# Pooled attention and a squared-ReLU layer: the first pair's fp32 scores of two heads in row halves, the weight conversion spread over three engines, one-piece splits and a new written order

## The chip, the cores and the metric

The kernel runs on one core of a Trainium2 chip. The metric is the device time of one execution in microseconds (us). The core has five engines that the text speaks of: PE (TensorE, matrix products), ACT (ScalarE), DVE (VectorE), POOL (GpSimd) and SP (SyncE, which here only starts DMA transfers). Each of them works through its own instructions in the order in which the program lists them.

## What is computed

```python
# q, k, v: (4, 8, 1152, 64); w_in: (512, 2048); w_out: (2048, 512); all float32
q_pool = q.reshape(B, H, S // 2, 2, D).mean(axis=3)
scores = scale * np.matmul(q_pool, k.transpose(0, 1, 3, 2))
scores = scores - np.max(scores, axis=-1, keepdims=True)
attn = np.exp(scores)
attn = attn / (np.sum(attn, axis=-1, keepdims=True) + 1e-09)
attn_out = np.matmul(attn, v)
x = attn_out.transpose(0, 2, 1, 3).reshape(B * 576, 512)   # 2304 tokens
r = np.maximum(x @ w_in, 0.0)
out = (r * r) @ w_out
```

## The kernel before

**Attention.** The 32 heads are worked on as 16 pairs, four pairs to a batch. A pair has 9 chunks of 128 query rows: four of each head, and one (the fifth) that holds the last 64 rows of both. There are 144 chunks, numbered from 0 in the order in which they are worked on. For a chunk `i` the steps are named: `S` (PE: scores, 128 x 1152, into one of two score tiles `s0` and `s1`, chosen by `i % 2`), `MX` (DVE: maximum of each row, L678), `EX` (ACT: exponential with row sums, L689 and L690, three instructions), and then the turning of the 128 x 1152 weights for the next product. In the first batch (chunks 0 to 35) that is `TP`, three groups of three transposes on PE (L738) into one of two PSUM banks `ba`, each followed by a copy out of the bank, `TC`, on ACT (L750) or DVE (L752). In the later batches a chunk is split into a high and a low fp16 part (`HI`, `LO`, L694 to L702) and turned by DMA (`TR`), or turned on PE (L788 to L811). `PV` multiplies with the values (L854 in fp32 for the first batch, L863 in fp16), and `ED` copies the result out.

**A pair's operands.** The keys and queries of a pair come by DMA (`LK`, `LQ`), get a scale (`GR`, `GM`, `GF`, `GS`, `GT`, `GU`, `GW`, `GE`), are split into fp16 parts (`KA` and `KD` for keys, `QA` and `QD` for queries, `VA` and `VD` for values), and are turned by DMA (`KT`, `QT`). `QX` (L588) copies the turned queries into the other half of the partitions, in two instructions of 64 partitions. `QS` adds neighbouring queries. Pair 0 alone is worked on in fp32: its keys and queries are turned on PE (`KX`, `QY`), and its scores are products with a contraction over 64 partitions, partitions 0 to 63 for the first head and 64 to 127 for the second (L649).

**Weights.** The two weight matrices are loaded in 16 pieces (`WL`, L1107) and converted, piece by piece, by bit operations: `W1` (L1113) and `W2` (L1118) on ACT, `W3` (L1122) and `W5` (L1126) on DVE, `W4` (L1135) on POOL or DVE. `WG`, `WM` and `WS1` to `WS3` find the scale of a matrix, `WA`, `WB` and `WD` split it into fp16 parts.

**The layer behind it.** When a block of 256 tokens is done, it is scaled and split (`RV` to `XD`) and goes through eight `H` (PE, L1005), with `HA`, `G1`, `G2`, `G3` on the other engines, and eight `O` (PE, L1054). There are nine blocks.

**The order.** Nothing is scheduled on the chip. A planner (class `Plan`) places all these steps one after the other on the five engines, from a table of durations, an offset for each kind of step and a few weights, all in `CFG` and `COST`. Where a step may go to two or three engines (`alt`, with the table `ALT`), the planner also picks the engine. The order that comes out is the program.

```python
ORD = [0, 1, 7, 8, 2, 3, 4, 5, 6]     # chunks of a pair: heads 0, 0, 1, 1, 0, 0, both, 1, 1
add(("S", i), {"PE": 2050}, ... + back, scores4, i)    # back: EX of chunk i - 2
add(("W1", c), {"ACT": 1030}, [("WL", c)] + wx, w1, at)
add(("QX", n), alt("QX", DVE=1100, POOL=2500), [("QT", n)] + old, qx, need)
```

## Time and profile before

| what | value |
|---|---|
| time of the kernel, median of 3 runs | 863.12 us (855.28 to 863.9) |
| time of the profiled execution | 867.78 us |
| its span, first to last instruction | 866.0 us |
| mean granted TensorE clock | 0.953 |
| PE busy | 786.8 us, 91% of the span |
| DVE busy | 629.5 us, 73% |
| ACT busy | 582.7 us, 67% |
| POOL busy | 373.4 us, 43% |

The span is 1.8 us shorter than the profiled execution's own time. That execution lies 4.7 us above the median of the runs. A share of busy time is a mean over the program: the chunks end at about 712 us, and behind that nearly only PE works. A clock of 1.00 in a stretch means that PE was granted 2.4 GHz, and 0.50 means 1.2 GHz. A busy time of PE at the lower level is longer for the same work.

### The profile page before, as it was taken

Reading aid. Unit: us, or ns where it says so; the run is one execution under the profiler, and the core shown is the slowest. Engines: PE = TensorE matmul, PEld = TensorE weight load, DVE = VectorE, ACT = ScalarE, POOL = GpSimd, SP = SyncE. Lnnn points to the kernel's source line nnn. Section 1 sums busy time; section 2 is a strip of 40 time slices with the busy share of each in tenths; the row PEclk is TensorE's granted clock in tenths of the full one; section 3 lists DMA queues with packets and bytes.
Section 4 is the critical chain, followed back from the end, with each engine's and each line's share of the span. In section 5 each row is a group of like instructions: output and inputs, shape, how many; then the busy total and the mean of one; then the engine's idle time right before and its main releaser. Section 6 shows DMA issues by size and latency. Waiting matters only on the chain. (4 is left out here: it accounts for less than half of the span.)

```text
span 866.0 us, 15480 instructions
## 1 busy us (share of the span) xinstructions
PE 786.8 (91%) x6106; PEld 517.2 (60%) x6106; DVE 629.5 (73%) x782; ACT 582.7 (67%) x953; POOL 373.4 (43%) x261
## 2 busy tenths in 40 slices
PE   6988878887799989898999898999989989999997
PEld 4555545454586557555765574577557646857573
DVE  2678999898978888888885988888888892413120
ACT  4567879599975678767884865588658872725150
POOL 2233332337676557444782556665357641000000
PEclk8669999898899999998999999899999999999999
DMA  9457953334787889797978987989989976000001
GB/s 286 126 139 193 251 164 125 85 98 93 125 150 149 169 180 184 150 196 135 203 123 187 195 159 161 181 153 179 171 175 182 183 136 108 2 13 13 13 13 25
DMA packets 296489, 120.72 MB, mean 139 GB/s; under 512 B 279776, under 2 KB 279776, under 8 KB 296416
## 3 DMA queue, kind: packets, MB, share of 16 engines
q1 hardware_dynamic: 296416, 119.73, 67.5%
q8 instruction: 48, 0.79, 0.4%
q14 instruction: 25, 0.20, 0.1%
HBM read 45.09 MB, written 4.72 MB: 58 GB/s over the span
## 5 line engine op out<-in xcount | busy, mean ns | idle before, releaser
L678 DVE TENSOR_REDUCE ca<-s 128x1 f32<-128x1152 f32 x144 | 193.0, 1349 | 28.4 <-PE s L670 17.4
L1005 PEld LDWEIGHTS <-w 128*128 128x128 f16 x1728 | 168.5, 98 | 31.4 <-issue 5.5
L690 ACT ACTIVATE buf<-s,ca,esc 128x1152 f32<-128x1152 f32 x135 | 177.0, 1311 | 6.9 <-POOL buf L702 0.3
L702 POOL TENSOR_TENSOR buf<-buf,buf 128x1152 f16<-128x1152 f32 x55 | 139.2, 2534 | 58.5 <-ACT buf L694 35.6
L1054 PE MATMUL ba<-w,region 128*128 128x512 f16 x672 | 153.3, 382 | 1.0 <-ACT ru L908 1.0
L670 PE MATMUL s<-kT,qT 128*128 128x512 f16 x720 | 138.9, 333 | 10.5 <-ACT buf L690 10.3
L1054 PEld LDWEIGHTS <-region 128*128 128x128 f16 x864 | 83.7, 99 | 96.8 <-issue 4.9
L1005 PE MATMUL ba<-region,w 128*128 128x256 f16 x1104 | 128.4, 275 | 2.4 <-DVE PT L811 1.8
L670 PEld LDWEIGHTS <-qT 128*128 128x128 f16 x720 | 64.9, 100 | 68.6 <-issue 21.3
L863 PE MATMUL ba<-PT,v 128*64 128x320 f16 (+1 forms) x1296 | 88.5, 296 | 6.3 <-DVE PT L811 3.2
L1032 DVE TENSOR_TENSOR region<-region 128x512 f16<-128x512 f32 x42 | 39.3, 936 | 69.3 <-ACT region L1025 68.7
L863 PEld LDWEIGHTS <-v 128*64 128x64 f16 x1296 | 74.6, 114 | 19.8 <-issue 12.6
L689 ACT ACTIVATE ca<-ca,cols,esc 128x1 f32<-128x1 f32 x135 | 51.4, 381 | 50.1 <-DVE ca L678 49.8
L702 DVE TENSOR_TENSOR buf<-buf,buf 128x1152 f16<-128x1152 f32 x41 | 64.7, 1578 | 9.6 <-ACT buf L694 5.9
L738 PE MATMUL ba<-ident,buf 128*128 128x128 f32 x324 | 56.8, 306 | 16.2 <-DVE PT L752 8.0
L349 POOL TENSOR_SCALAR buf<-buf,cols 128x1152 f16<-128x1152 f32 x31 | 43.6, 1407 | 52.8 <-ACT buf L690 36.7
L352 DVE SCALAR_TENSOR_TENSOR buf<-raw,psc,buf 128x576 f16<-128x576 f32 x45 | 55.7, 1272 | 3.4 <-POOL buf L326 3.4
L738 PEld LDWEIGHTS ba<-ident,buf 128*128 128x128 f32 x324 | 37.8, 153 | 33.5 <-DVE PT L752 13.7
L1032 POOL TENSOR_TENSOR region<-region 128x512 f16<-128x512 f32 x30 | 42.4, 1414 | 34.0 <-ACT region L1025 31.8
L750 ACT ACTIVATE PT<-ba 128x384 f32<-128x384 f32 (+1 forms) x73 | 31.1, 454 | 27.5 <-PE ba L738 27.0
L1005 PE MATMUL bt<-region,w 128*128 128x256 f16 x432 | 49.2, 273 | 0.0
L1135 POOL TENSOR_TENSOR w<-w,region 128x1024 f32<-128x1024 f32 x11 | 26.5, 2410 | 52.2 <-DVE w L1126 50.0
(158 smaller groups left out, 1112.0 us busy)
## 6 DMA issues: line engine op xcount, KB each, us to landing
raw<-in_k_dram SPq DMA_DIRECT2D x16, 576.0 KB, 4.6
raw<-in_q_dram SPq DMA_DIRECT2D x32, 288.0 KB, 4.4
region<-in_moe_w_in_dram SPq DMA_DIRECT2D x8, 1024.0 KB, 6.0
region<-in_moe_w_out_dram SPq DMA_DIRECT2D x8, 1024.0 KB, 5.4
raw<-in_v_dram SPq DMA_DIRECT2D x12, 576.0 KB, 4.5
out_dram<-buf SPq DMA_DIRECT2D x36, 128.0 KB, 2.4
v<-in_v_dram SPq DMA_DIRECT2D x4, 576.0 KB, 5.5
PT<-buf SPq DMA_TRANSPOSE x108, 4.8
```

Source lines behind the costliest of these rows:

```text
L349: nc.gpsimd.tensor_scalar(out, x, s0, s1, op0=ALU.mult, op1=ALU.mult)
L352: nc.vector.scalar_tensor_tensor(out=o, in0=x, scalar=s, in1=h, op0=ALU.mult, op1=ALU.subtract)
L670: nc.tensor.matmul(s[:, x, :w], lhsT=qt[:, l, h, c0 : c0 + 2, :].rearrange("p a b -> p (a b)"), rhs=rhs, **st)
L678: nc.vector.reduce_max(a[:, 0:1], st3(), axis=AX.X)
L689: nc.scalar.activation(a[:, 1:2], a[:, 0:1], AF.Identity, bias=ln14, scale=s0)
L690: nc.scalar.activation(P(), st3(), AF.Exp, bias=a[:, 1:2], scale=s1, accum_out=col)
L702: e.tensor_tensor(out=hl()[:, 1], in0=P(), in1=hl()[:, 0], op=ALU.subtract)
L738: nc.tensor.matmul(t[:, y], lhsT=P()[:, c * 128 : (c + 1) * 128], rhs=ident, is_transpose=True, start=(y == 0), stop=(y == 2), skip_group_ ...
L863: nc.tensor.matmul(px[h * 64 : (h + 1) * 64, :N], lhsT=vv[:, h, kc, vl, :], rhs=t[:, 9 * pl + kc, :N], start=(i == 0), stop=(i == 3 * NC - ...
L1005: nc.tensor.matmul(ph[:, f2], lhsT=w16[0][:, SLOT[f // 4], wl, a, f % 4 * 128 : (f % 4 + 1) * 128], rhs=xhl()[:, xl, a], start=(i == 0), s ...
L1032: e.tensor_tensor(out=gt[u][:, 1], in0=rt[u % 2], in1=gt[u][:, 0], op=ALU.subtract)
L1054: nc.tensor.matmul(p[:, :DM], lhsT=g[:, gl, f % 2, tt * 128 : (tt + 1) * 128], rhs=w16[1][:, SLOT[f // 4], wl, f % 4], start=(f == 0 and g ...
```

## The change

**Scores of pair 0.** The chunks of pair 0 are taken in the order `ORD4`, in which each two neighbours belong to different heads, and one `S` now computes two chunks: its matrix products alternate between partitions 0 to 63, into `s0`, and 64 to 127, into `s1`. The fifth chunk stays alone. The joint `S` waits for the `EX` of two earlier chunks, since it writes both score tiles.

**Weight conversion.** `W1` may go to ACT or POOL, `W2` to ACT or DVE. On DVE `W2` is a bit operation on 16-bit words.

**Splits.** `KD`, `VD` and `QX` were steps of two instructions each; each instruction is now a step that is placed by itself, and the two halves of a `QX` may go to different engines.

**Order.** `CFG` and `COST` hold other numbers, so the planner's whole order is another one. The rest of the diff (operands kept in a buffer, `PART`, visits) is not used with this `CFG`.

How many steps of a kind stand on an engine, where the two programs differ by three or more:

| step | before | after |
|---|---|---|
| `S` of pair 0 | PE 9 | PE 5 |
| `W1` | ACT 16 | POOL 16 |
| `W2` | ACT 16 | ACT 12, DVE 4 |
| `W4` | POOL 14, DVE 2 | POOL 11, DVE 5 |
| `TC` | ACT 65, DVE 43 | ACT 83, DVE 25 |
| `QX`, instructions | DVE 30 | DVE 15, POOL 15 |
| `KA` | POOL 11, ACT 4 | POOL 4, ACT 11 |
| `VA` | ACT 8, POOL 4 | ACT 3, POOL 9 |
| `HI` | ACT 41, POOL 31, DVE 24 | ACT 44, POOL 24, DVE 28 |
| `G2` | ACT 49, POOL 13, DVE 10 | ACT 64, POOL 2, DVE 6 |
| `G3` | DVE 42, POOL 30 | DVE 27, POOL 45 |
| `ED` | ACT 23, DVE 9 | ACT 20, DVE 12 |

```diff
-ALT = {"TC": "D", "KC": "D", ...}
+ALT = {"W1": "P", "W2": "D", "TC": "D", "KC": "D", ...}
...
+    def both(i):
+        n, _, vi = chunks[i]
+        if n not in full_s:
+            return (i,)
+        x = i - visits[vi][2]
+        y = i if x == 4 else i - (x - (x > 4)) % 2
+        return (i,) if x == 4 else (y, y + 1)
...
         def scores4(o):
-            s = sts[i % 2]
...
-                nc.tensor.matmul(
-                    s[:, x, :w], lhsT=qt[hs, cs].rearrange("p a b -> p (a b)"),
-                    rhs=kt[hs, k0:k1].rearrange("p a b -> p (a b)"), start=True, stop=True,
-                )
+                for y in both(i):
+                    ch = CH[chunks[y][1]]
...
+                    nc.tensor.matmul(
+                        sts[y % 2][:, x, :w], lhsT=qt[hs, cs].rearrange("p a b -> p (a b)"),
+                        rhs=kt[hs, k0:k1].rearrange("p a b -> p (a b)"), start=True, stop=True,
+                    )
...
         if n in full_s:
-            add(("S", i), {"PE": 2050}, ... + back, scores4, i)
+            if both(i)[0] == i:
+                back = [("EX", y - 2) for y in both(i) if y >= 2]
+                add(("S", i), {"PE": 2200 if len(both(i)) == 2 else 2050}, ... + back, scores4, i)
...
-            add(("KD", n), {"DVE": 1500}, [("KA", n)], kd, need, give=("k", n))
+            for h in range(2):
+                add(("KD", n, h), {"DVE": 730}, [("KA", n)] + ..., lambda o, h=h: kd(o, h), need, ...)
...
-            add(("QX", n), alt("QX", DVE=1100, POOL=2500), [("QT", n)] + old, qx, need)
+            for z in range(2):
+                add(("QX", n, z), alt("QX", DVE=470, POOL=1500), [("QT", n)] + old, lambda o, z=z: qx(o, z), need)
...
                     def w1(o, w=w, i=i, half=half, c=c):
-                        nc.scalar.activation(
-                            f32(w, i)[:, half], wst[c % 2][:, :, :, 1].bitcast(F32), AF.Copy, scale=2.0 ** -112
-                        )
+                        to, x = f32(w, i)[:, half], wst[c % 2][:, :, :, 1].bitcast(F32)
+                        if o["eng"] == "ACT":
+                            nc.scalar.activation(to, x, AF.Copy, scale=2.0 ** -112)
+                        else:
+                            pmul(to, x, 2.0 ** -112)
 
                     def w2(o, c=c):
-                        nc.scalar.activation(wsg[c % 2], wst[c % 2][:, :, :, 1].bitcast(F32), AF.Sign)
+                        if o["eng"] == "ACT":
...
+                            e.tensor_scalar(
+                                wsg[c % 2].bitcast(I16), wst[c % 2].bitcast(I16)[:, :, :, 3], -(2 ** 15), 0x3F80,
+                                op0=ALU.bitwise_and, op1=ALU.bitwise_or,
+                            )
...
-                    add(("W1", c), {"ACT": 1030}, [("WL", c)] + wx, w1, at)
+                    add(("W1", c), alt("W1", ACT=1030, POOL=1250), [("WL", c)] + wx, w1, at)
...
+    ORD4 = [0, 7, 1, 8, 4, 2, 5, 3, 6]
```

Three places show how the order moves. The first is PE at the start: `L442` is the last of the queries' turning, `s0_113` and `s1_114` are the two score tiles, and the rows behind are the first scores. Before:

```order
L442 MATMUL ba0_115<-ident_81,raw1_101 64x64 x8
L649 MATMUL s0_113<-kT0_102,qT0_104 128x512 x2
L649 MATMUL s0_113<-kT0_102,qT0_104 128x128
L649 MATMUL s1_114<-kT0_102,qT0_104 128x512 x2
L649 MATMUL s1_114<-kT0_102,qT0_104 128x128
```

After, where `L677` is the same line:

```order
L459 MATMUL ba0_115<-ident_81,raw1_101 64x64 x8
L677 MATMUL s0_113<-kT0_102,qT0_104 128x512
L677 MATMUL s1_114<-kT0_102,qT0_104 128x512
L677 MATMUL s0_113<-kT0_102,qT0_104 128x512
L677 MATMUL s1_114<-kT0_102,qT0_104 128x512
L677 MATMUL s0_113<-kT0_102,qT0_104 128x128
L677 MATMUL s1_114<-kT0_102,qT0_104 128x128
```

The two tiles were filled one after the other by two steps; they are now filled in turn by one.

The second is DVE about chunk 14, in the first batch: `L588` and `L604` are `QX`, `L1122` and `L1161` are `W3`, `L1126` and `L1165` are `W5`, `L1135` is `W4`, `L678` and `L706` are `MX`, `L356` is a half of `KD`. Before:

```order
L588 COPY qT_104<-qT_104 64x1152 x2
L521 TENSOR_SCALAR psc<-psc 128x2
L1126 SCALAR_TENSOR_TENSOR region<-region 128x1024
L528 TENSOR_SCALAR psc<-psc 128x2
L1135 TENSOR_TENSOR region<-region 128x1024
L534 RECIPROCAL psc<-psc 128x2
L1166 TENSOR_REDUCE wsc<-ba_115 128x1
L678 TENSOR_REDUCE ca<-s_114 128x1
```

After:

```order
L706 TENSOR_REDUCE ca<-s_113 128x1
L356 SCALAR_TENSOR_TENSOR buf_97<-raw_101,psc,buf_97 128x9x64
L706 TENSOR_REDUCE ca<-s_114 128x1
L1161 TENSOR_SCALAR region<-region 128x1024
L604 COPY qT_104<-qT_104 64x1152
L1165 SCALAR_TENSOR_TENSOR region<-region 128x1024
```

One of the two copies of `QX` has left DVE here, `W4` has left it in this place, and a half of `KD` stands between two `MX`.

The third is POOL from the first `QS` (`L407` and `L423`) on: `L353` with a `w` behind it is `W1`, `L1135` and `L1174` are `W4`, `L349` is `GE`, `L326` is `KA` and `QA`, `L604` is a half of `QX`. Before:

```order
L407 TENSOR_TENSOR raw_101<-raw_101 128x9x64
L1135 TENSOR_TENSOR w_0_90<-w_0_90,region 128x1024
L407 TENSOR_TENSOR raw_101<-raw_101 128x9x64
L349 TENSOR_SCALAR esc<-psc 128x1 x2
L326 TENSOR_SCALAR buf_96<-raw_100,psc 128x18x64
L326 TENSOR_SCALAR buf_97<-raw_101,psc 128x9x64
L1135 TENSOR_TENSOR w_0_90<-w_0_90,region 128x1024 x3
```

After:

```order
L423 TENSOR_TENSOR raw_101<-raw_101 128x9x64
L353 TENSOR_SCALAR w_0_90<-region 128x1024
L1174 TENSOR_TENSOR w_0_90<-w_0_90,region 128x1024
L353 TENSOR_SCALAR w_0_90<-region 128x1024
L423 TENSOR_TENSOR raw_101<-raw_101 128x9x64
L353 TENSOR_SCALAR w_0_90<-region 128x1024
L353 TENSOR_SCALAR esc<-psc 128x1 x2
L1174 TENSOR_TENSOR w_0_90<-w_0_90,region 128x1024
L353 TENSOR_SCALAR w_0_90<-region 128x1024 x2
L1174 TENSOR_TENSOR w_0_90<-w_0_90,region 128x1024
L604 COPY qT_105<-qT_105 64x1152
```

The first pieces of `W1` and a half of `QX` now stand between `QS`, `GE` and `W4`; `KA` and `QA` of pair 1 have left POOL.

## Rows read from the trace of the kernel before

**Rows 1.** By stretch: us; busy of PE, PEld, DVE, ACT, POOL; PEclk; DMA; GB/s:

```profile
0.00:58.95 58.95, 49.61 (x224) 30.29 (x224) 29.73 (x44) 30.32 (x52) 16.81 (x19) 0.74 0.69 202
58.95:194.96 136.01, 113.31 (x894) 72.59 (x891) 124.97 (x174) 110.72 (x184) 46.75 (x31) 0.96 0.54 146
194.96:712.25 517.29, 476.34 (x3891) 316.37 (x3890) 437.43 (x504) 385.07 (x630) 304.15 (x200) 0.96 0.87 163
712.25:866.00 153.75, 147.55 (x1105) 97.95 (x1103) 37.42 (x64) 56.57 (x91) 5.70 (x11) 0.99 0.15 29
```

**Rows 2.** PE in order of time: start us, us, what, at the first pair:

```profile
11.14 4.14 PE L649 MATMUL s<-kT,qT 64*128 64x512 f32 x12
19.02 4.21 PE L649 MATMUL s<-kT,qT 64*128 64x512 f32 x6
41.62 2.10 PE L649 MATMUL s<-kT,qT 128*128 128x512 f32 x6
64.49 4.36 PE L854 MATMUL ba<-PT,v 128*64 128x256 f32 x36
```

**Rows 3.** Two 3 us stretches of the first pair, columns as in group 1:

```profile
24.00:27.00 3.00, 3.00 (x6) 1.25 (x5) 1.26 (x5) 1.98 (x4) 1.57 (x3) 0.50 0.02 10
39.00:42.00 3.00, 2.67 (x16) 1.74 (x16) 3.00 (x5) 2.97 (x6) 0.71 (x1) 1.00 0.86 324
```

**Rows 4.** ACT in order of time, the first exponential:

```profile
14.96 0.30 ACT L689 ACTIVATE ca<-ca,cols 128x1 f32<-128x1 f32 x1 [0.98 <-DVE ca L678]
15.29 1.22 ACT L690 ACTIVATE buf<-s,ca 128x1152 f32<-128x1152 f32 x1
```

**Rows 5.** Groups of DVE in the second stretch: busy us, mean ns, idle before:

```profile
L678 DVE TENSOR_REDUCE ca<-s 128x1 f32<-128x1152 f32 x29 | 39.1, 1352 | 7.0 <-PE s L670 6.1 <-PE s L665 0.5 <-ACT ca L689 0.2
L752 DVE COPY PT<-ba 128x384 f32<-128x384 f32 (+1 forms) x34 | 16.3, 513 | 3.5 <-ACT xm L324 3.4
L1126 DVE SCALAR_TENSOR_TENSOR w<-region,w 128x1024 int32<-128x1024 int32 x8 | 10.5, 1309 | 0.0
L588 DVE COPY qT<-qT 64x1152 f16<-64x1152 f16 x8 | 8.2, 1029 | 0.2
L1122 DVE TENSOR_SCALAR w<-w 128x1024 int32<-128x1024 int32 x8 | 7.4, 926 | 0.0
L1166 DVE TENSOR_REDUCE wsc<-ba 128x1 f32<-128x512 f32 x8 | 5.4, 680 | 0.2 <-PE ba L1160 0.2
L1135 DVE TENSOR_TENSOR w<-w,region 128x1024 f32<-128x1024 f32 x1 | 1.2, 1226 | 0.1
```

**Rows 6.** Groups of ACT in the second stretch:

```profile
L750 ACT ACTIVATE PT<-ba 128x384 f32<-128x384 f32 (+1 forms) x57 | 24.1, 454 | 10.9 <-PE ba L738 10.7
L1118 ACT ACTIVATE region<-region 128x1024 bf16<-128x1024 f32 x12 | 13.7, 1139 | 0.0
```

**Rows 7.** Groups of POOL in the second stretch:

```profile
L1135 POOL TENSOR_TENSOR w<-w,region 128x1024 f32<-128x1024 f32 x7 | 17.4, 2479 | 25.1 <-DVE w L1126 22.9 <-DVE psc L521 2.2
L326 POOL TENSOR_SCALAR buf<-raw,psc 128x1152 f16<-128x1152 f32 (+1 forms) x7 | 7.6, 1090 | 0.3
```

**Rows 8.** What PE waited for in the second stretch: us, times, longest:

```profile
PE ba L738 <- DVE PT L752: 6.2, 7, 1.7
```

**Rows 9.** Two lines of DVE over the program: ns shortest/median/longest:

```profile
L588 DVE COPY qT<-qT x30: 452/456/2536, 52.6 to 672.3; 64x1152 f16<-64x1152 f16 x30
L1122 DVE TENSOR_SCALAR w<-w x12: 666/690/2632, 13.0 to 135.2; 128x1024 int32<-128x1024 int32 x12
```

**Rows 10.** Groups of DVE in the third stretch:

```profile
L698 DVE CAST buf<-buf 128x1152 f16<-128x1152 f32 x24 | 29.1, 1212 | 8.1 <-ACT buf L690 5.3 <-issue 2.5
L1032 DVE TENSOR_TENSOR region<-region 128x512 f16<-128x512 f32 x19 | 23.4, 1231 | 8.4 <-ACT region L1025 7.8 <-POOL region L1028 0.3
L1028 DVE TENSOR_TENSOR region<-region 128x512 f32<-128x512 f32 x10 | 12.3, 1232 | 3.3 <-ACT region L1020 3.3
L588 DVE COPY qT<-qT 64x1152 f16<-64x1152 f16 x20 | 15.7, 786 | 4.0 <-DMA qT<-buf 3.7
```

More of the change, by code (lines that the diff above doesn't have):

```diff
@@ L370, in prep @@
         need = preps[n]["need"] if n else cfg("P0", -1000)
-        slot = preps[n]["slot"]
         p0 = preps[n]["old"]
-        old = [("S", preps[p0]["last"])] if p0 is not None else []
-        oldv = [("PV", *preps[p0]["lastg"])] if p0 is not None else []
+        old = [("S", both(preps[p0]["last"])[0])] if p0 is not None else []
+        keep = preps[n]["slot"] is None
+        vs = preps[n]["visits"]
+        slot = vs[0] % 2
+        oldvs = [[("PV", vi - 2, lastr[vi - 2])] if vi >= 2 else [] for vi in vs]
+        oldv = oldvs[0]
         def rk():
@@ L399, in prep @@
         if n in full_v:
-            add(("LV", n), {"SP": 2500}, oldv, lambda o: load_kv(v4(slot), v), need, after=[("LQ", n)])
+            for y, vi in enumerate(vs):
+                add(("LV", n, vi), {"SP": 2500}, oldvs[y], lambda o, vi=vi: load_kv(v4(vi % 2), v), need if y == 0 else visits[vi][2], after=[("LQ", n)])
         else:
@@ L637, in st3 @@
             return sts[i % 2].rearrange("p a b -> p (a b)")[:, :1152]
+        end = preps[n]["slot"] is None and i == preps[n]["last"]
         def scores4(o):
-            s = sts[i % 2]
-            kt, qt = k4(slot), q4(slot)
+            kt, qt = k4(n), q4(qT(n))
             for x in range(3):
@@ L1269 @@
     for n, p in enumerate(preps):
-        before = [m for m in range(n) if preps[m]["slot"] == p["slot"]]
+        before = [m for m in range(n) if p["slot"] is not None and preps[m]["slot"] == p["slot"]]
         p["old"] = before[-1] if before else None
@@ L1299 @@
         nc.vector.tensor_scalar(pick, pick, 2.0 ** -14, None, op0=ALU.mult)
-        for i in range(2):
-            nc.gpsimd.memset(q4(i)[:, 9:11], 0.0)
+        for t in qTs if full_s else ():
+            nc.gpsimd.memset(q4(t)[:, 9:11], 0.0)
         for o in seq:
```

119 lines of the change are left out of this document (58 added, 61 removed), and 9 rows, old and new, of the table COST.

## The prediction

> **What bounds the kernel now.** I read the busy time by stretch first, then the groups of the busiest engine in each stretch, then who PE waits for, then single instructions.
>
> I cut the span where the row maxima of chunks 9, 36 and 143 start [rows 1]. In the first 58.95 us (pair 0) PE is busy for 49.61 us, but at a mean granted clock of 0.74, so part of that time is slow work. Why can be seen in single rows. The first two score steps ran at the full level, 12 records in 4.14 us, and the third took 4.21 us for 6 records [rows 2]. From 24 to 27 us PE was busy without a gap and was still granted 0.50 (1.2 GHz), while it did half-array scores and transposes; from 39 to 42 us, ahead of and in the one full-array score step, it was granted 1.00 (2.4 GHz) [rows 3], and that step took 2.10 us [rows 2]. So PE is the bound of the first stretch, at the low level.
>
> In the second stretch (136.01 us, 27 chunks) DVE is busy for 124.97 us, 92%; ACT has 81%, PE 83%, POOL 34% [rows 1]. DVE is its bound. PE's largest wait there is for copies by DVE, 6.2 us [rows 8], and 10.7 us of ACT's idle time is a wait for PE's transposes [rows 6], so neither of them sets the pace.
>
> In the third stretch (517.29 us) PE is busy for 476.34 us, 92%, DVE for 437.43 us, 85%. In the last (153.75 us) PE has 96% [rows 1]. There PE is the bound, and its work is given: what is saved ahead of it moves the end by as much, if the third stretch still finds PE its work.
>
> **The change, part by part.**
>
> *Pair 0's scores.* Before, nine steps: eight half-array ones of 2.07 us at the high level (4.14 for two) to 4.21 us at the low one, and one full-array step. Now four joint steps and the single one. What a joint step costs is not in the trace, since no two products in different row halves stand side by side there. The ends: 2.1 us, if both halves run at once at the high level, and 8.4 us, if they run one after the other at the low one (2 x 4.21). The nearest row is the fp32 product with the values, whose products lie alternately in two column halves of the array: 18 products of 256 columns, 4608 columns, in 4.36 us, against two score steps of 512, 512 and 128 columns, 2304 in all, in 4.14 us [rows 2]. So two column halves do run beside each other, at twice the columns in the same time. I take the same for row halves, 2.1 to 4.2 us for a joint step at the high or the low level: the halves use different rows of the array and different score tiles.
>
> The Trainium skill (TensorEngine Tiling (Array Packing), Theoretical Speedup) gives up to 2x for a contraction of at most 64. By it a joint step would cost one step's 2.07 us at the high level; no row here shows it.
>
> The joint step adds a wait: it needs both score tiles, so the exponentials of both earlier chunks. On PE the transposes, WG and PV are queued behind it. A pair of chunks is then a chain: step (2.1 to 4.2), maximum 1.35 [rows 5], two exponentials of about 1.6 each with the bias instruction (0.30 and 1.22 and the gap, [rows 4]), three handovers of some 0.2, in all 7.2 to 9.3 us. From the first score step at 11.14 I walk: second exponential done at 18.2; the second joint step, done through its exponentials, at 25.5 to 27.6; the single step starts at 24.8 to 26.9 and is done through its exponential at 30.3 to 34.3; now PE goes first through WG of the first piece and the first PV (4.36 us [rows 2], twice that at the low level), so that the third joint step starts at 37 to 46; the fourth ends its first exponential at 50 to 63. Only then is a score tile free for chunk 9. Its maximum falls at 51 to 64, against 58.95; I take 57.5. Also the operands of pair 1 must be there: KT and QT now stand on SP behind two more weight loads, and half of QX goes to POOL. Their DVE parts stand ahead of MX 5, about 37 us, and before, QX of pair 1 began at 52.6 [rows 9] with nothing of PE waiting for it, so these 15 us are their cover. Term: -1.5 us, between -8 and +5. PV and two WG are done besides, which the second stretch no longer has to do.
>
> *DVE in the second stretch.* I counted the steps that stand on DVE between MX 9 and MX 36 in both programs. TC: 31 to 18, -13 x 0.513 = -6.7. Copies of QX: 8 to 3, -5 x 1.029 = -5.1. W3: 12 to 10, -1.9. W5: 12 to 11, -1.3. WM: 8 to 6, -1.4. MX: one less, -1.4. W4: 2 to 4, +2 x 1.226 = +2.5. W2: 0 to 3; no row has it; its ends are W3's 0.926 (the same number of elements, one input) and W5's 1.309, I take W3's: +2.8 [rows 5]. Halves of KD and VD: the same instructions as before in smaller steps, 0. Sum -12.5 us of 125.0. If DVE stays 92% busy, the stretch takes 112.5 / 0.919 = 122.4 us: -13.6.
>
> What could be next there: ACT loses 11 W1 and 4 W2 (each like the 1.139 of W2) and two each of WA and WB, and takes 8 TC at 0.454 [rows 6], so it falls too. PE loses a PV, two WG and a few transposes, about 9 us of 113.3. POOL takes 10 W1 and 3 halves of QX and gives off, above all, two KA and three W4. W1 on POOL is not in the trace; its ends are 1.09 (KA and QA, one input) and 2.479 (W4, two inputs) [rows 7]; I take 1.2, as W1 has one input and the 1.09 has QA's half-length ones in it. That makes 13 x 1.2 = +16 against -2.4 and -7.4: little for a queue that is 34% busy. GE and QS now stand behind W1 there; the chunks that need them come a pair later, which covers a few us.
>
> *Third stretch.* ACT gets two WA and two WB (4 x 2) and some 18 G2 more, a few per cent on its 74%. DVE: G3 -10 x 1.231, G2 -8 x 1.232, copies of QX -9 x 0.786, HI +4 x 1.212, one LO more: about -23 of 437 us, 5% [rows 10]. PE has one O more (2.6) and three TP less. PE's idle 41 us are in small waits; if they shrink like DVE's work, by 5%, that is -2; the ends are -8 and +4. In the last stretch one O less stands against the one more: 0.
>
> *Sum*: -1.5 - 13.6 - 2 = -17.1 us on the profiled 867.8, so 850.7. That execution is 0.5% above the median; on 863.1 it is 846.1. I say 846.
>
> **The rivals** (against the median of 863).
>
> *DVE isn't what sets the second stretch.* A chunk takes 5.0 us there, and its chain through score, maximum, exponential, transposes and copies in two banks could set that pace by itself. For it: DVE's 11 us of idle time are mostly waits for scores (6.1 us, [rows 5]). Against it: these are short, and DVE is never empty for long. Then the stretch keeps its 136: 863 - 3.5 = 860, no change.
>
> *POOL holds DVE up (slower).* Some DVE instructions take far longer than their median: the QX copy 0.456 and up to 2.536, W3 0.690 and up to 2.632 [rows 9]; a hold by POOL would look like that. Suppose that each new POOL step holds a DVE step for its full length, and that those taken off had held none: 7 x 1.2 = 8.4 us in the first stretch, of which perhaps half lies on the chain; 13 x 1.2 = 15.6 us on DVE in the second (128.1 / 0.919 = 139.4, +3.4); and 11 more halves of QX in the third, 13 us, undo its gain and add some 4. With -1.5 + 4.2 + 3.4 + 4 = +10 that is 873, slower. Between this and the forecast lie 27 us, so it turns into a loss when more than 17 / 27 = 0.6 us of DVE is lost per us of added POOL work. In the rows, QX loses 8 x (1.029 - 0.456) = 4.6 and W3 8 x (0.926 - 0.690) = 1.9 us in a stretch with 46.75 us of POOL [rows 1, 5, 9]: 0.14 per us, and with the other kinds perhaps 0.2. The Trainium skill (SBUF — State Buffer, Who interferes with whom) says of the pair of ports shared by the two engines that "the other fully blocks". The longest rows agree with that, and the medians say that it mostly does not come to it.
>
> *The halves don't overlap* (the change does not do what it says): the joint steps cost 4.2 to 8.4 us, chunk 9's maximum falls at up to 72, +13.5, which eats the second term: 861, no change.
>
> *PE sets the second stretch, as in the third*: its remaining 104.3 us at 92% are 113.4 us, -22.6; with the early end of the first term (-8) and -4 for the third stretch, 829.
>
> **How the numbers follow.** Chances: forecast 0.52 (838 to 855), chain in place of DVE 0.17, POOL 0.10, halves 0.10, PE 0.11. A measurement of this kernel tells about 1% from no change. Faster by over 1% (below 854.5): nearly all of the forecast, the PE case and a part of the mixed cases, 0.67; slower by over 1% (above 871.7): POOL and the worst of the halves, 0.11; within 1%: 0.22. The range from 829 to 866 takes in the forecast, the PE case, the chain case and the middle of the halves.
>
> **What would show it.** In the profile of the changed kernel: joint score steps of 12 records in 2.1 to 4.3 us; chunk 9's maximum at 51 to 64 us; chunk 36's at about 180 instead of 195; DVE at about 112 us of busy time between them, at 0.9 or more of the stretch; chunk 143's maximum at about 695 instead of 712; a last stretch of 154 us. I am wrong if the second stretch keeps its 136 us with DVE less busy, if W3, W5 or QX get longer in the mean, or if the third stretch grows by what the second gives.

## The result and the profile after

| | median | lowest to highest |
|---|---|---|
| before, same chip | 863.13 us | 855.28 to 863.9 |
| after, 4 runs | 826.38 us | 822.9 to 829.35 |

The ratio is 0.9592 (95% interval 0.9524 to 0.9661): faster by 37 us where 17 were forecast, and below the range of 829 to 866. The profiled execution took 827.69 us, its span is 825.9 us.

The same four stretches of after, cut where the maxima of chunks 9, 36 and 143 start; columns as in [rows 1], to which they answer:

```profile
0.00:59.21 59.21, 42.04 (x311) 29.28 (x312) 37.02 (x49) 32.67 (x64) 24.66 (x24) 0.91 0.74 219
59.21:181.76 122.55, 102.54 (x810) 65.42 (x809) 112.20 (x146) 98.53 (x182) 48.20 (x38) 0.99 0.51 149
181.76:676.10 494.34, 466.19 (x3918) 310.80 (x3918) 405.84 (x490) 398.99 (x640) 310.42 (x207) 0.98 0.93 173
676.10:825.90 149.80, 144.99 (x1076) 95.96 (x1071) 37.34 (x63) 53.45 (x85) 9.13 (x15) 0.99 0.14 27
```

| stretch | before | after | difference | forecast |
|---|---|---|---|---|
| first | 58.95 | 59.21 | +0.3 | -1.5 |
| second | 136.01 | 122.55 | -13.5 | -13.6 |
| third | 517.29 | 494.34 | -23.0 | -2 |
| last | 153.75 | 149.80 | -4.0 | 0 |

The first two lines came out almost to the number, DVE's 112.20 us in the second too. The miss is in the third: PE was busy for 10.2 us less there (476.34 to 466.19) and idle for 12.8 us less (41.0 to 28.2). The shorter busy time is the clock: the granted clock averaged 0.964 in before's third stretch and 0.983 in after's. By these two means 18.6 and 8.4 us were lost to the lower level (an estimate: 0.036 x 517 and 0.017 x 494), a difference of 10.

PE of after in order of time, as in [rows 2]:

```profile
11.47 2.21 PE L677 MATMUL s<-kT,qT 64*128 64x512 f32 x12
...
17.60 4.26 PE L677 MATMUL s<-kT,qT 64*128 64x512 f32 x12
...
34.50 4.11 PE L884 MATMUL ba<-PT,v 128*64 128x256 f32 x36
```

A joint step has 12 records in 2.21 us at the high level and 4.26 at the low one, where one step of a single chunk took 2.07 and 4.21. So the row halves do run beside each other, as the column halves had suggested. The Trainium skill (TensorEngine Tiling (Array Packing), Theoretical Speedup) gives up to 2x here; 4.14 us for two steps against 2.21 is 1.87x.

Groups of DVE in the second stretch of after, as in [rows 5]:

```profile
L1165 DVE SCALAR_TENSOR_TENSOR w<-region,w 128x1024 int32<-128x1024 int32 x7 | 11.4, 1639 | 0.1
...
L1165 DVE SCALAR_TENSOR_TENSOR region<-region 128x1024 int32<-128x1024 int32 x4 | 6.9, 1728 | 0.1
...
L1161 DVE TENSOR_SCALAR w<-w 128x1024 int32<-128x1024 int32 x7 | 4.7, 682 | 1.3 <-POOL w L353 1.3
```

`W5` (L1165) is longer than the 1.309 us of before and `W3` (L1161) shorter than its 0.926. The 11 `W5` cost 18.3 us where 11 x 1.309 = 14.4 had been reckoned; the seven `W3` 4.7 where it was 6.5. `W2` on DVE cost 1.29 us each, where 0.93 had been taken. These errors of +4, -2 and +1 do not show in the sum, because others offset them: that it met the forecast so closely is in part luck. `W1` on POOL, from the same stretch's POOL groups:

```profile
L353 POOL TENSOR_SCALAR w<-region 128x1024 f32<-128x1024 f32 x6 | 8.2, 1371 | 4.6 <-DMA region<-in_moe_w_out_dram 3.6 <-DVE ca L706 1.0
...
L353 POOL TENSOR_SCALAR region<-region 128x1024 f32<-128x1024 f32 x4 | 4.5, 1128 | 4.0 <-DMA region<-in_moe_w_in_dram 3.1 <-DMA region<-in_moe_w_out_dram 0.9
```

That is 1.27 us in the mean, near the 1.2 taken. Groups of DVE in the third stretch of after, answering to [rows 10]:

```profile
L726 DVE CAST buf<-buf 128x1152 f16<-128x1152 f32 x28 | 24.6, 879 | 12.3 <-ACT buf L718 12.2
...
L604 DVE COPY qT<-qT 64x1152 f16<-64x1152 f16 x11 | 9.3, 847 | 3.9 <-DMA qT<-buf 3.5
...
L1062 DVE TENSOR_TENSOR region<-region 128x512 f16<-128x512 f32 x9 | 6.2, 687 | 6.1 <-ACT region L1055 4.8 <-POOL region L1058 1.2
...
L1058 DVE TENSOR_TENSOR region<-region 128x512 f32<-128x512 f32 x2 | 2.3, 1138 | 0.0
```

Not only are there fewer `G3` (L1062) and `G2` (L1058): one `G3` took 687 ns in the mean instead of 1231, one `HI` (L726) 879 instead of 1212. DVE lost 31.6 us here where 23 had been counted.

The steps themselves did not become cheaper. `HI` on DVE in the third stretch, before and after, in ns shortest/median/longest:

```profile
L698 DVE CAST buf<-buf x24: 747/760/2861, 201.1 to 706.9; 128x1152 f16<-128x1152 f32 x24
...
L726 DVE CAST buf<-buf x28: 739/760/1970, 204.7 to 668.7; 128x1152 f16<-128x1152 f32 x28
```

The median is the same; before has more long ones. Take as the short length of a kind of step the tenth percentile over the profiles. Then 76 DVE steps of before's third stretch ran over 0.25 us longer than that, by 88 us in all, and 63 of after's, by 63 us. Every one of them ran beside a step of POOL. At their short lengths the steps add up to 370 us before and 362 after. So (an estimate) some 7 of the 31.6 us are less work, and 25 are steps that were held up less beside POOL, although POOL was as busy as before (304 and 310 us). One such case, in after, first DVE's `LO`, then POOL's `WD`, then PE:

```profile
189.13 5.14 DVE L730 TENSOR_TENSOR buf<-buf,buf 128x1152 f16<-128x1152 f32 x1
...
188.99 4.07 POOL L1255 TENSOR_TENSOR w<-w 128x2048 f16<-128x2048 f32 x1 [0.65 <-ACT w L1251]
...
196.14 0.29 PE L932 MATMUL ba<-negid,r 128*32 128x128 f16 x1 [4.34 <-DVE r L928]
```

The `LO` starts 0.14 us behind the `WD` and ends 1.21 us behind its end; it took 5.14 us where the median of its kind is 1.36. PE's longest wait for DVE in after, 4.34 us, is for a step that stands behind it.

What PE waited for tells where its idle time went. The waits of PE for DVE in the third stretch of before (us, times, longest):

```profile
PE ba L788 <- DVE PT L811: 3.9, 6, 1.2
...
PE ba L788 <- DVE x L937: 3.5, 1, 3.5
PE ba L863 <- DVE PT L811: 3.2, 1, 3.2
...
PE ba L788 <- DVE buf L1068: 2.2, 1, 2.2
```

and the same of after:

```profile
PE ba L932 <- DVE r L928: 4.3, 1, 4.3
PE ba L818 <- DVE PT L841: 3.3, 3, 2.5
PE ba L768 <- DVE PT L782: 2.1, 2, 1.2
```

With the smaller rows, PE's waits for DVE make 24.7 us before and 12.3 after; those for ACT are 15.9 and 15.6. In nearly all of before's waits for DVE, PE wants one of the two `ba` banks, and DVE has not yet read it out; so it is in after, but for the 4.3 us of L928. One such place, DVE of before at 538 us:

```profile
537.86 0.80 DVE L352 SCALAR_TENSOR_TENSOR buf<-raw,psc,buf 128x576 f16<-128x576 f32 x1
538.58 1.34 DVE L678 TENSOR_REDUCE ca<-s 128x1 f32<-128x1152 f32 x1
539.85 0.80 DVE L1068 TENSOR_SCALAR buf<-ba,os 128x512 f32<-128x512 f32 x1
```

and PE there:

```profile
537.99 0.55 PE L788 MATMUL ba<-ident,buf 128*128 128x128 f32 x3 [0.98 <-DVE PT L811]
540.70 0.90 PE L788 MATMUL ba<-ident,buf 128*128 128x128 f32 x3 [2.17 <-DVE buf L1068]
```

The copy that frees the bank takes 0.80 us, but a `QD` and a row maximum stand ahead of it, and PE idles 2.17 us. In the wait of 3.45 us for L937, in before at 404 us, part of what stands ahead is a step held up beside POOL, a `GU` on two numbers a partition, whose median is 0.16 us:

```profile
399.99 2.23 DVE L528 TENSOR_SCALAR psc<-psc 128x2 f32<-128x2 f32 x1
...
399.83 2.36 POOL L702 TENSOR_TENSOR buf<-buf,buf 128x1152 f16<-128x1152 f32 x1 [4.82 <-ACT buf L694]
```

What such a gap costs besides shows in four windows of before around this wait; the third number from the right is the granted clock:

```profile
396.00:400.00 4.00, 4.00 (x28) 2.05 (x25) 2.91 (x6) 2.95 (x4) 0.17 (x1) 1.00 1.12 207
400.00:404.00 4.00, 0.89 (x13) 0.34 (x9) 3.96 (x4) 1.55 (x2) 2.72 (x3) 0.87 0.47 90
404.00:408.00 4.00, 3.49 (x12) 1.90 (x13) 4.00 (x7) 2.81 (x6) 1.82 (x1) 0.50 0.88 144
408.00:412.00 4.00, 4.00 (x55) 3.52 (x55) 1.95 (x3) 2.99 (x5) 2.58 (x2) 0.78 1.23 204
```

PE idles for 3.1 us in the second window and is granted 0.50 in the third and 0.78 in the fourth: of its 7.5 us of busy time there, 3.49 x 0.50 + 4.00 x 0.22 = 2.6 are lost to the clock. This one gap was paid nearly twice.

### The profile page after: what moved, and what is told of

The parts are those of the page before. It is cut to its first block, busy times and chain, and to the rows that moved or that the text cites. A ratio compares the mean times of both kernels' runs of the same rounds, so it can differ in the third digit from the quotient of the medians.

```text
span 825.9 us, 15535 instructions
## 1 busy us (share of the span) xinstructions
PE 755.8 (92%) x6106; PEld 501.5 (61%) x6106; DVE 592.4 (72%) x745; ACT 583.6 (71%) x967; POOL 392.4 (48%) x284
## 5 line engine op out<-in xcount | busy, mean ns | idle before, releaser
L706 DVE TENSOR_REDUCE ca<-s 128x1 f32<-128x1152 f32 x144 | 192.7, 1349 | 34.2 <-PE s L677 16.6
L730 POOL TENSOR_TENSOR buf<-buf,buf 128x1152 f16<-128x1152 f32 x53 | 129.3, 2441 | 46.4 <-ACT buf L722 25.9
L1084 PE MATMUL ba<-w,region 128*128 128x512 f16 x624 | 141.8, 379 | 0.2 <-DVE PT L841 0.2
L1062 POOL TENSOR_TENSOR region<-region 128x512 f16<-128x512 f32 x45 | 62.8, 1397 | 102.3 <-ACT region L1055 98.4
L893 PE MATMUL ba<-PT,v 128*64 128x320 f16 (+1 forms) x1296 | 84.2, 287 | 0.5 <-ACT ru L938 0.5
L768 PE MATMUL ba<-ident,buf 128*128 128x128 f32 x324 | 52.5, 289 | 19.3 <-ACT buf L718 9.3
L780 ACT ACTIVATE PT<-ba 128x384 f32<-128x384 f32 (+1 forms) x93 | 39.2, 455 | 30.2 <-PE ba L768 29.1
L1050 ACT ACTIVATE region<-region 128x512 f16<-128x512 f32 x72 | 45.0, 626 | 19.1 <-PE bt L1084 16.2
L356 DVE SCALAR_TENSOR_TENSOR buf<-raw,psc,buf 128x576 f16<-128x576 f32 x45 | 52.7, 1199 | 2.9 <-ACT buf L328 1.7
L1084 PE MATMUL bt<-w,region 128*128 128x512 f16 x240 | 53.8, 379 | 0.0
L722 ACT ACTIVATE buf<-buf 128x1152 f16<-128x1152 f32 x44 | 51.1, 1161 | 1.8
L1062 DVE TENSOR_TENSOR region<-region 128x512 f16<-128x512 f32 x27 | 18.7, 691 | 46.3 <-ACT region L1055 44.7
```

Of the source, the lines that this page charges most:

```text
L356: nc.vector.scalar_tensor_tensor(out=o, in0=x, scalar=s, in1=h, op0=ALU.mult, op1=ALU.subtract)
L706: nc.vector.reduce_max(a[:, 0:1], st3(), axis=AX.X)
L722: nc.scalar.activation(hl()[:, 0], P(), AF.Copy)
L730: e.tensor_tensor(out=hl()[:, 1], in0=P(), in1=hl()[:, 0], op=ALU.subtract)
L768: nc.tensor.matmul(t[:, y], lhsT=P()[:, c * 128 : (c + 1) * 128], rhs=ident, is_transpose=True, start=(y == 0), stop=(y == 2), skip_group_ ...
L893: nc.tensor.matmul(px[h * 64 : (h + 1) * 64, :N], lhsT=vv[:, h, kc, vl, :], rhs=t[:, 9 * pl + kc, :N], start=(i == 0), stop=(i == 3 * NC - ...
```

## The experiments

Fifteen kernels ran, one of them before itself again. "In after's order" is after with an edit, "in before's order" before with one. The table gathers the third stretch of each profile, cut for all at the 37th maximum in time (in before that is chunk 37's, 2.3 us ahead of chunk 36's): its length, PE's busy time, the difference, PE's waits for DVE (the rows of the waits summed), and DVE's busy time, all in us. The number in brackets leaves out one wait, explained below the table.

| kernel | third stretch | PE busy | PE idle | waits for DVE | DVE busy |
|---|---|---|---|---|---|
| before | 519.6 | 478.5 | 41.1 | 24.7 | 439.7 |
| e10, before again | 520.1 | 478.7 | 41.5 | 23.6 | 443.9 |
| e13, PE's gap filled | 521.4 | 480.0 | 41.4 | 23.4 | 444.1 |
| e14, copies early | 524.0 | 475.9 | 48.1 | 27.1 | 447.0 |
| e8, G2 and G3 moved | 518.0 | 476.8 | 41.2 | 22.1 | 414.2 |
| e12, QX moved too | 512.9 | 473.9 | 39.0 | 20.6 | 409.5 |
| e4, old numbers | 526.2 | 483.9 | 42.3 | 20.2 | 405.0 |
| after | 494.3 | 466.2 | 28.2 | 12.3 | 405.8 |
| e1, halves apart | 491.0 | 464.7 | 26.4 | 12.5 | 403.6 |
| e3, W1 and W2 on ACT | 491.2 | 466.6 | 24.6 | 9.1 | 402.0 |
| e7, QX on DVE | 493.4 | 468.8 | 24.6 | 12.2 | 408.5 |
| e11, more G3 on POOL | 491.7 | 466.5 | 25.2 | 10.9 | 401.6 |
| e16, e1 and e11 | 494.0 | 467.2 | 26.8 | 17.5 (11.8) | 403.5 |
| e6, pieces together | 499.8 | 470.8 | 29.0 | 17.7 (12.1) | 406.9 |
| e15, copies late | 503.0 | 470.2 | 32.8 | 19.5 | 403.4 |
| e2, G2 and G3 back | 506.0 | 470.1 | 36.0 | 19.4 | 426.2 |
| e9, three undone | 516.6 | 475.6 | 41.0 | 26.7 (21.0) | 437.2 |

In every profile of after's order PE stands for some 5.4 us at the same `GF` (L528), about 30 us into the third stretch. The profile puts this wait down to whichever step came last, ACT's in after and most others, DVE's in e6, e9 and e16. Here are after and e6:

```profile
PE ba L528 <- ACT buf L718: 5.4, 1, 5.4
...
PE ba L528 <- DVE region L967: 5.6, 1, 5.6
```

So it is left out in brackets. Where the third stretch is the same (after, e1 and e3), it took 491.0 to 494.3 us and the waits were 9.1 to 12.5; before, e10 and e13 are as close to each other.

### The first two stretches

**e1: the halves apart.** In after, the joint step does all of the first tile and then all of the second.

```diff
-            for x in range(3):
-                k0, k1 = 4 * x, min(4 * x + 4, 9)
-                w = 128 * (k1 - k0)
-                for y in both(i):
+            for y in both(i):
+                for x in range(3):
+                    k0, k1 = 4 * x, min(4 * x + 4, 9)
+                    w = 128 * (k1 - k0)
```

> The changed kernel with one edit: each joint score step of pair 0 does all products of the first tile and then all of the second, at the same place in the same order. Theory (halves in turn run beside each other): each of the four joint steps goes from 2.2 to about 4.2 us, more at the low clock, chunk 9's maximum moves from 59 to 67 to 75 us and the end moves by as much, 834 to 842 us. Rival (the chain of exponentials and DVE covers the score step, so the saved PE time of the first stretch is worth little): under 3 us later, 826 to 829.

Measured: 824.58 us, ratio 0.9605 (0.954 to 0.967). The step in e1, from PE in order of time:

```profile
11.01 3.17 PE L677 MATMUL s<-kT,qT 64*128 64x512 f32 x12
...
17.64 5.98 PE L677 MATMUL s<-kT,qT 64*128 64x512 f32 x12
```

Alternating saves 1 to 1.7 us a step, and none of it reaches the end: chunk 9's maximum starts at 59.62 instead of 59.21. So it came out as the rival said. In the first stretch of after, PE idles for 17 us anyway. Apart, 3.17 us is still less than two steps (4.14), so some of the overlap needs no alternation.

**e3: W1 and W2 all back on ACT**, in after's order.

```diff
     seq = plan.order(("EX", NSTEP - 1))
+    MOVE = {("W1", 0): "ACT", ("W1", 1): "ACT", ...}
+    for o in seq:
+        o["eng"] = MOVE.get(o["name"], o["eng"])
```

> The changed kernel with its order kept, but all 16 W1 and all W2 back on ACT. This gives ACT some 23 us more in the first two stretches (98.5 of 122.6 us busy in the second), POOL 19 us less, DVE 3 us less. Theory (the move of W1 and W2 freed ACT to take the copies of the transposes, which is what made DVE's part in the second stretch smaller): the second stretch grows, 6 to 15 us, 832 to 841. Rival (POOL's new work holds DVE, so taking it off helps): 820 to 826.

Measured: 834.54 us, 0.9724 (0.9653 to 0.9794), as the theory said. Its second stretch:

```profile
61.04:190.94 129.90, 105.29 (x809) 67.12 (x808) 104.90 (x143) 110.99 (x195) 35.08 (x28) 0.96 0.52 142
```

It grew by 7.3 us, with 12.5 us more on ACT and DVE lighter by 7.3. So `W1` on POOL and the four `W2` on DVE are together worth about 7 of the 13.5 us that the second stretch gained; the rest was not taken apart. There ACT's load counts as well as DVE's: DVE is at 81% here, yet the stretch is longer. Of DVE's 7.3 us three `W2` are 3.9; the other 3.4 are steps that were shorter with 13.1 us less work on POOL, `W5` above all (1.35 us in its larger group instead of 1.64). That is near the spread: in e11, whose second stretch has after's steps and places, DVE is busy for 109.1 us.

**e10: before once more**, with no line changed.

> The kernel of before once more, for a second profile. Theory 1 (the first stretch varies with the clock it is granted, the third does not depend on it): the first 9 chunks take between 47 and 59 us, by the clock; PE's waits for DVE in the third stretch are again 24 to 25 us in all, and that stretch is again 515 to 520 us. Theory 2 (the 59 us and the 517 us of the first profile are properties of the order): both come out as before within 1 us.

Measured: 868.08 us, one run. The first stretch took 57.97 us, the third 520.1: both as in the first profile. The two theories part only with the first stretch of e8 (below, the same instructions of the same order up to there) and of e13. The first stretches of e12 and e14, also in before's order, took 49.5 and 50.5 us at 0.90 and 0.88.

**e13: PE's gap filled**, in before's order.

```diff
                 t = raw(nm, n).bitcast(BF16).rearrange("p (f t) -> p f t", t=2)[:, :, 1]
+                if (n, nm) == (1, "q"):
+                    t1 = raw("k", n).bitcast(BF16).rearrange("p (f t) -> p f t", t=2)[:, :, 1]
+                    for c in range(24):
+                        x = t1[:, (c % 9) * 128 : (c % 9) * 128 + 128]
+                        nc.tensor.matmul(p[:, 0], lhsT=x, rhs=x, start=True, stop=True)
```

> Before, with 24 extra products of pair 1's keys on PE at about 16 us, where PE waits about 2 us for the next pair's queries; their result is overwritten, the output is the same. Theory 1 (the 58 to 59 us of the first stretch against 46.8 come of the clock that falls at 17 to 18 us, after this gap): PE has no gap there, the first 9 chunks take 47 to 50 us in nearly every execution, and the median is 852 to 856. Theory 2 (the fall has nothing to do with the gap): the first stretch stays at 55 to 60 us and the median at 861 to 866.

Measured: 860.0 us (855.79 to 862.71, 12 runs), ratio 0.9971 (0.9936 to 1.0005): at most a small gain, against the 852 to 856 of the first theory. In the one profile the first stretch took what that theory said. Here it is in e10, e8 and e13, a fence for each:

```profile
0.00:57.97 57.97, 48.71 (x224) 29.50 (x224) 29.97 (x44) 29.47 (x50) 16.98 (x19) 0.76 0.69 204
```

```profile
0.00:46.79 46.79, 35.88 (x224) 22.77 (x224) 29.80 (x44) 29.31 (x50) 16.98 (x19) 1.00 0.84 253
```

```profile
0.00:46.83 46.83, 36.96 (x248) 23.92 (x248) 29.79 (x44) 29.30 (x50) 17.01 (x19) 1.00 0.86 253
```

The same 224 products took 48.71 us of PE at a mean clock of 0.76 and 35.88 at 1.00. So before's first stretch is anything from 47 to 59 us by the clock alone. But the gap is not shown to make the clock fall. e8, e12 and e14 have it too (1.36, 1.22 and 0.98 us), and the clock did not fall there: in e8 it stayed at 1.00 through the stretch, in e12 and e14 until about 38 us. In before and e10 it fell at gaps of 2.07 and 1.16 us; e13 itself kept a gap of 0.74 us. Of the 11 us by which e13's is shorter than e10's, its second and third stretch give back 2.3 and 1.3; why the median gained only 4 stays open.

### The third stretch

**e2: G2 and G3 back** on the engines of before, in after's order (53 steps; net 19 more on DVE).

```diff
+    MOVE = {..., ("G3", 0, 0): "DVE", ("G3", 0, 1): "DVE", ("G2", 0, 2): "DVE", ...}
+    for o in seq:
+        o["eng"] = MOVE.get(o["name"], o["eng"])
```

> The changed kernel with its order kept, but every G2 and G3 on the engine that it had before (net 15 G3 and some 5 G2 more on DVE, about 20 us of DVE work, nearly all in the third stretch). Theory A (the third stretch got 23 us shorter because DVE has less to do there, so that PE waits less and falls less often to the low clock): the third stretch grows by 10 to 20 us, the time is 836 to 846. Rival B (it got shorter by where the new order places the work, whatever DVE carries): within 4 us of 826.

Measured: 836.21 us, 0.9737 (0.9677 to 0.9797). The third stretch of e2:

```profile
182.39:688.42 506.03, 470.05 (x3921) 312.40 (x3921) 426.19 (x508) 387.38 (x621) 311.42 (x208) 0.98 0.91 169
```

DVE got 20.3 us more, PE's waits for DVE grew by 7.1, the stretch by 11.7: half the gain. This adds work and also puts it ahead of other steps in DVE's queue, so it does not part amount from place.

**e7: the 15 QX halves back on DVE**, and **e6: the pieces of KD, VD and QX behind each other again**, both in after's order, e7 by a `MOVE` as above, e6 by

```diff
+    half_ = {o["name"]: o for o in seq if o["name"][0] in ("KD", "VD", "QX")}
+    out_, done_ = [], set()
+    for o in seq:
...
+        if o["name"] in half_:
+            other = o["name"][0], o["name"][1], 1 - o["name"][2]
+            out_.append(half_[other])
+            done_.add(other)
+    seq = out_
```

> The changed kernel with its order kept, but the 15 halves of QX that went to POOL back on DVE (11 of them in the third stretch, some 5 to 9 us of DVE work there, 14 us less on POOL). Theory A (DVE's amount of work counts): 2 to 6 us slower, 828 to 832, nearly all of it in the third stretch. Rival (POOL's hold on DVE costs as much as the work itself): within 2 us of 826.

> The changed kernel with the two pieces of every KD, VD and QX put directly behind each other again, as they stood before; engines and all other places are kept. Theory A (DVE's amount of work counts): within 4 us of 826. Rival C (the third stretch got shorter since a row maximum no longer waits behind two pieces of 0.8 to 2.9 us each): the third stretch grows by 6 to 20 us, 832 to 846.

Measured: e7 826.68 us, 0.9633 (0.9572 to 0.9694), no effect, as the rival said: DVE got 11 copies back in the third stretch, 5.0 us at their median of 0.456, and is busy for 2.7 us more (408.5). Equal third stretches of after's order differ by more than that (402.0 to 405.8), so whether DVE was held up less in return is not shown.

e6 830.51 us, 0.966 (0.9603 to 0.9716), an interval that overlaps after's. DVE's work is the same (406.9) and only places in a queue changed; the stretch grew by 5.5 us, which is beyond the spread of equal stretches. But PE's waits for DVE did not grow (12.1 and 12.3), and its idle time grew by 0.8 us only. The rest is 4.6 us of busy time, at a mean granted clock of 0.976 instead of 0.983.

**e9: all three undone**, in after's order.

```diff
+    MOVE = {..., ("G2", 0, 2): "DVE", ("G2", 0, 3): "DVE", ..., ("QX", 1, 1): "DVE", ...}
...
+    seq = out_
```

> The changed kernel with three things undone at once, its order otherwise kept: G2 and G3 on the engines of before, QX wholly on DVE, and the pieces of KD, VD and QX behind each other. Theory A with C as a smaller part: the three add up, +10 (G2 and G3), +4 (pieces), +2 to +6 (QX), 842 to 847, with a third stretch of 512 to 518, that is nearly all that it had before. Rival B (a good part lies in the place of the work): the third stretch stays under 508.

Measured: 848.76 us, 0.9887 (0.9821 to 0.9954); the third stretch is 516.6 us, DVE 437.2. That takes back 22 of the 25 us, as theory A had it, and more than e2, e6 and e7 one by one (12 + 5 + 0).

**e8: G2 and G3 as in after, in before's order**, and **e12: one QX copy of each pair on GpSimd besides.**

```diff
+    MOVE = {..., ("G3", 0, 0): "POOL", ("G3", 0, 1): "POOL", ("G2", 0, 2): "ACT", ...}
...
-            for a, b_ in ((0, 64), (64, 0)):
+            for z, (a, b_) in enumerate(((0, 64), (64, 0))):
+                e = nc.gpsimd if (n, z) in QXP else nc.vector
```

> The kernel before with its order kept, but every G2 and G3 on the engine that the changed kernel gives it: some 20 us less on DVE. Theory A: its third stretch (517 us) gets shorter by 8 to 15 us, 848 to 855 in all. Rival B (the place counts): within 4 us of 863.

> Before, with G2 and G3 on the engines of after and one of the two QX copies of each pair on GpSimd, as in after. DVE's work in the third stretch falls from 437 to about 405, as light as after's. If the amount of DVE's work sets PE's waits: these fall from 24.7 to about 13 us, the third stretch to about 495, and the time to about 840. If the order for which the assignment was made decides: PE's waits for DVE stay above 20 us, the third stretch at 512 to 520, and the time at 858 to 868.

Measured: e8 866.06 us, 1.0044 (0.998 to 1.0108); e12 858.29 us, 0.9962 (0.9913 to 1.001): no clear gain in either. The third stretch of e12:

```profile
185.64:698.54 512.90, 473.88 (x3904) 313.75 (x3904) 409.51 (x478) 395.44 (x652) 310.55 (x210) 0.98 0.88 165
```

DVE is as light as in after, to 4 us, and PE still waits 20.6 us for it, 18.6 us of stretch more than after. In e12's waits, `ba <- x` with 3.4 us and `ba <- buf` with 2.2 stand at the same places as L937 and L1068 in before. A lighter DVE alone is not it. The pieces of `KD`, `VD` and `QX` apart as well, in before's order, were not tried.

**e4: after's code with the old `CFG`, `COST` and `LOCK`.** `LOCK` is the planner's list of the DVE steps that it starts only behind POOL's; the change adds `W2`, `GT`, `GU` and `XT` to it.

```diff
-CFG = {..., 'WSP': 0.6478, 'WOF': 20.5281, 'MSP': 18.4869, ...}
+CFG = {..., 'WSP': 1.0134, 'WOF': 11.344, 'MSP': 13.8824, ...}
```

> The changed kernel's structure (joint score steps, W1 and W2 free to move, single pieces) with the planner's numbers of the kernel before (CFG, COST and the list of steps that wait for POOL). The planner makes another order and other engine choices of it. Theory (most of the third stretch's gain comes from what the new numbers choose: G2, G3 and QX off DVE): 845 to 870, its third stretch above 505. Rival (the structure alone gives the gain): 820 to 835.

Measured: 886.24 us, 1.0325 (1.0245 to 1.0404), slower than before. The time is beyond both expectations. PE has 4006 products in the third stretch against 3918, so not all of its length is order. But DVE is as light as in after (405.0), PE waits 20.2 us for it, and the stretch is the longest of all. That steps may go to more engines, and as pieces, gains nothing with the numbers of the old order.

**e14 and e15: only places on DVE.** In before's order the steps that empty a bank behind `O` and `RB` (L1068, L937) stand up to two places earlier; in after's order the same ones (L1098, L967) up to two later (`d + 2`, `d + 1` and `to + 0.5` in the lines below).

```diff
...
+        if o["name"][0] in ("OD", "XR") and a < i < b:
...
+            for to in (dve[d - 2], dve[d - 1]):
...
+                    key[i] = to - 0.5
...
+    seq = [seq[i] for i in sorted(range(len(seq)), key=lambda i: key[i])]
```

> Before, with one thing changed on DVE's queue in the third stretch: the steps that empty a bank of PE behind O and behind RB (L1068 and L937) stand up to two places earlier, no step changes its engine. If the place in the queue sets PE's waits: the 9.4 us that PE waits there for L1068 and L937 fall below 4, PE's waits for DVE from 24.7 to about 18, the third stretch from 517 to 503 to 510, and the time to 849 to 857. If DVE's amount of work sets them: the waits turn up behind other steps of DVE, 22 to 26 us in all, and the stretch stays at 515 to 520, the time at 861 to 866.

> After, with the same steps (L1098 and L967) up to two places later on DVE's queue in the third stretch, no step on another engine. If the place decides: PE's waits for DVE grow from 12.3 to 16 to 20 us, the third stretch from 494 to 500 to 510, and the time to 832 to 842. If the amount of work decides: no change, 824 to 829.

Measured: e15 834.75 us, 0.969 (0.9625 to 0.9755), as the place would have it. New waits for these very copies in e15:

```profile
PE ba L818 <- DVE buf L1098: 3.0, 2, 1.9
...
PE ba L893 <- DVE buf L1098: 2.7, 2, 1.8
```

PE's waits for DVE went from 12.3 to 19.5 us, PE's busy time from 466.2 to 470.2 and the stretch by 8.6, at 2 us less DVE work.

e14: 874.42 us (863.59 to 879.11), 1.0098 (1.0049 to 1.0148), slower, where one theory expected a gain and the other no change. The waits for L1068 and L937 fell from 9.4 to 3.6 us, as meant, but those for L811 rose from 8.9 to 17.3. One place, DVE of e14:

```profile
393.30 0.81 DVE L1068 TENSOR_SCALAR buf<-ba,os 128x512 f32<-128x512 f32 x1 [1.42 <-POOL buf L702]
394.02 1.35 DVE L678 TENSOR_REDUCE ca<-s 128x1 f32<-128x1152 f32 x1
395.29 4.54 DVE L352 SCALAR_TENSOR_TENSOR buf<-raw,psc,buf 128x576 f16<-128x576 f32 x3
399.75 1.01 DVE L811 TENSOR_TENSOR PT<-ba,PT 128x384 f16<-128x384 f32 x2
```

and PE behind it:

```profile
400.35 0.90 PE L788 MATMUL ba<-ident,buf 128*128 128x128 f32 x3 [4.66 <-DVE PT L811]
```

The other bank's copy (L811) now stands behind a `QD` and two `KD` halves, 4.54 us, of which one half took 2.91 beside a `LO` on POOL. In e14 DVE also waits 4.2 us for `O` to end, in four places, with all else behind it. So the place counts, but "earlier" is not by itself the better one. The profiled execution was among e14's shortest (865.07 us), so its 524.0 us show only a part of the 10 us by which the median is slower.

**e11 and e16: further than after.** e11 gives the nine `G3` that DVE keeps in the third stretch to POOL; e16 is e1 and e11 together.

```diff
+    MOVE = {("G3", 0, 2): "POOL", ("G3", 1, 2): "POOL", ("G3", 1, 7): "POOL", ...}
```

> After, with the nine G3 that are left on DVE in the third stretch given to POOL. Amount and placement together: DVE loses 9 x 0.69 = 6.2 us there; when G2 and G3 went back, 20.3 us more of DVE made 7.1 us more waiting of PE for DVE and 12 us more of stretch, so now PE's waits for DVE fall from 12.3 to about 10, the third stretch from 494 to about 490.5, and the time to about 823. Placement alone: a step given to an engine for which the order was not made gains nothing or costs; POOL gets 9 x 1.43 = 12.9 us, PE's waits stay at 12 or grow, and the time is 826 to 832.

> The two edits of after that came out a little below it, together: the joint step does the first tile and then the second, and the nine G3 are on POOL. If the small differences are real they add up: 819 to 823. If they are chance: 824 to 828.

Measured: e11 826.62 us, 0.9571 (0.9526 to 0.9616); e16 827.69 us, 0.9616 (0.9556 to 0.9676). Neither differs from after; e11's third stretch is 2.6 us shorter, too little to tell. No version that was tried is faster than after by what can be measured.

## Why the prediction was wrong

**First stretch: right in number, on an uncertain base.** Joint steps cost 2.21 to 4.26 us (2.1 to 4.2 said), chunk 9's maximum fell at 59.21 (51 to 64, 57.5 taken). But 58.95 us was one execution at a clock of 0.74. The prediction looked for the reason in the half-array products; e8 did the same products at 1.00, so they alone are not the reason. Against e8 (1.00) the 37th maximum comes at 181.6 us in before's order and at 181.8 in after's: the first two stretches together then gain nothing. Against the profiled execution of before (192.6) they gain 11. After's first stretch does more of the work (311 products against 224) and took 57 to 65 us in all ten profiles of its order. Before's runs lay between 851 and 872 us beside the experiments, after's own between 823 and 829. Even the shortest of before lies 25 us above after's median, about what the third and the last stretch alone gained (27).

**Second stretch: right in number**, 122.55 against 122.4, DVE's busy time 112.20 against 112.5, in part by errors that offset each other. e3 shows that moving `W1` and `W2` off ACT made about half of the gain, and that the account was too narrow in calling DVE its only bound.

**Third stretch: here the prediction failed.** Its step was "PE's idle 41 us are in small waits; if they shrink like DVE's work, by 5%, that is -2; the ends are -8 and +4". Measured: -23.0. Three things stood wrong in it.

- The idle time does not shrink in proportion to a load. PE's waits for DVE went from 24.7 to 12.3 us, while DVE's busy time fell by 7%. e8 and e12, with DVE lightened by 26 to 30 us in an order that was not made for it, remove only 3 to 4 us of these waits. e15, with DVE's work unchanged, adds 7 through places alone.
- PE's busy time was held fixed ("its work is given"). It fell by 10 us, the time by which the clock was granted more. This does not follow the idle time at a fixed price: e12 idles for 39.0 us at a clock of 0.98, e14 for 48.1 at 0.97, before for 41.1 at 0.96.
- DVE's work was priced by means that held the time lost beside POOL. It fell by 31.6 us, not 23, and by the estimate above only 7 of them are fewer steps. This matters least, since e12 has a DVE as light as after's.

So neither the amount nor the place alone explains it: in after's order the assignment of `G2` and `G3` counts (e2, 12 us), in before's order it hardly does (e12, 7 us with `QX`), and e9 says that assignment and pieces together make up 22 of the 25. How these 22 divide between the steps and an order that was made for them is not shown. What remains (3 us) is of the size by which e1 and after differ (491.0 and 494.3), which are the same from chunk 9 on. Which of the order's many numbers produced the good places was not tried.

**Last stretch**: PE's busy time fell by 2.6 us, one `O`, as counted; but the `O` that was to be paid for ahead of it found room in the third stretch. The other 1.4 us were idle time.

**Rivals.** "POOL holds DVE up" was wrong in the time, but not in the mechanism, and one sign that the prediction named came: `W5` grew by 0.3 to 0.4 us each in the second stretch, and in the third the mean `QX` on DVE went from 0.79 to 0.85. In the second stretch e3 prices it at no more than 0.26 us per us of POOL's work (3.4 for 13.1, near the spread), against the 0.14 to 0.2 said and the 0.6 that would have made a loss. In the third stretch it went the other way: DVE lost 25 us less beside POOL than before. "The halves don't overlap" and "DVE isn't what sets the second stretch" fell with 2.21 and 122.55 us, the latter with the reservation of e3. "PE sets the second stretch" gave 829, nearest to the result, by the wrong place.
